# Issue order in a fused attention and two-MoE kernel: casts queued behind bank-emptying additions, and one block's loads on another queue

## The chip, the cores and the metric

The kernel runs on one core of a Trainium2 chip. The core has five instruction streams that run side by side and meet only at semaphores: PE (TensorE, matrix multiplies into PSUM banks), DVE (VectorE), ACT (ScalarE), POOL (GpSimd) and SP (which here only issues DMA transfers). Each stream is served strictly in its own order: an instruction that waits holds up all that stand behind it on that stream. The metric is the time of one execution in microseconds, of which the median of a few runs is shown. A run of this kernel can be told from another when they differ by about 0.2%.

## The reference

Three stages follow one another: attention with rotary embedding over 4 batches of 8 heads, 576 tokens and width 64; a first MoE block; a second one. Only the second matters here:

```python
def _moe2_ref(x, w_in, w_out):          # x: 2304 x 512, w_in: 512 x 2048, w_out: 2048 x 512
    h = x @ w_in
    g = h * (1.0 / (1.0 + np.exp(-h)))
    return (g @ w_out).astype(np.float32)
```

## The kernel before

Every float32 matrix is held as two float16 parts, a high one (`h`, an ACT cast with a scale) and a low one (`l`, what the cast left over, made by DVE's scalar_tensor_tensor from the source and `h`). A product is three passes: high by high, high by low, low by high.

The second MoE (`moe2`, from line 871) takes the 2304 tokens in 9 blocks of 256, numbered `jb` 0 to 8. Block 0 is alone: `s1(u)` computes its hidden values with plain products, for four units u of 512 hidden values. Blocks 1 and 2, 3 and 4, 5 and 6, 7 and 8 go in pairs, J = 0 to 3 (`A` is the odd block, `B` the even one). For a pair, `s1_pair(J, p)`, p = 0 to 7, forms a 2 by 2 block product with seven multiplications (`PRODUCTS`) in place of eight. Their inputs are seven linear forms of x, cast into the tile `yr` by `y7_forms`; form b is written over tile place b from place b + 1, so that the forms can only be made one after another. Seven products of six passes each are 42 matmuls of 256 columns, into four PSUM banks a, b (ring `m`) and c, d (ring `mb`).

Then the banks are emptied: ACT copies one half of b and one half of c (lines 953 and 957), DVE makes six additions and POOL one (lines 952 and 960), and ACT applies SiLU in place (line 964). Until the additions that read a bank are done, the next step can't write to it.

`second(jb, u)` is the product with w_out for one unit, again 42 matmuls (`s2`, line 1010). It needs the unit's hidden values in seven forms: `g_split` makes four sums on POOL (`gsum`, line 893) and two casts each on ACT (line 897) and DVE (line 898). `splits()` calls `g_split` for units that are complete, up to three ahead of the next `second`. After the four units of a block, `close(jb)` combines and stores it.

For each J the next pair's operands are brought in meanwhile: `y7_load(J + 1)` (four DMAs of 256 KB out of the scratch `yscr`, traced in step p = 0), `y7_max` (the greatest magnitude, one DVE reduction, line 150, p = 1), `y7_sums` (the scale, by two small PE operations and a row of small DVE ones, and four POOL differences, line 981; p = 2), `y7_forms` (p = 3 to 7). For J = 0 all this stands in the loop over `s1`.

The order of each engine's instructions is not the order of the program text. A planner simulates the kernel and lets each engine take, at each moment, a ready instruction, the earliest traced one first. `tc.issue_after(ins)` binds the instructions traced inside it: those on the engine of `ins` stand behind `ins` in that engine's order. It adds no wait for the end of `ins`. On its own, a cast whose input is ready early may be set ahead of the additions of a step that was traced before it.

Of the kernel before, what the change touches and what calls it, by code (L numbers as in the profile page):

```python
# [7 lines left out]
F32 = mybir.dt.float32  # L8
# [3 lines left out]
AF = mybir.ActivationFunctionType  # L12
ALU = mybir.AluOpType
# [4 lines left out]
P = 128  # L18
# [4 lines left out]
def fused_kernel(  # L23
# [22 lines left out]
    nc = tc.nc  # L46
# [102 lines left out]
    def absmax(out, in_):  # L149
        nc.vector.tensor_reduce(out=out, in_=in_, op=ALU.max, axis=AX.X, apply_absolute_value=True)  # L150

    def flat(t):
        return t.rearrange("p a b -> p (a b)")

    def split(h, l, x, s, engine="act", later=False):

        if engine == "act":
            nc.scalar.activation(out=h, in_=x, func=AF.Copy, scale=s)  # L158
        elif engine == "pool":
            last["pool"] = nc.gpsimd.tensor_scalar(out=h, in0=x, scalar1=s, scalar2=1.0, op0=ALU.mult, op1=ALU.mult).ins  # L160
        else:
            nc.vector.tensor_scalar(out=h, in0=x, scalar1=s, scalar2=None, op0=ALU.mult)
        low = lambda: nc.vector.scalar_tensor_tensor(out=l, in0=x, scalar=s, in1=h, op0=ALU.mult, op1=ALU.subtract)
        return low if later else low()
# [3 lines left out]
    class Weights:  # L168
# [12 lines left out]
        def place(self, pool):  # L181
            n, m, nm = self.n, self.m, self.nm
            self.first = pool.tile([P, n], F16, name=nm + "f")
            self.all = pool.tile([P, m * n], F32, name=nm)
            self.t = [self.all[:, i * n:(i + 1) * n] for i in range(m)]
# [63 lines left out]
    last = {}  # L249
# [241 lines left out]
    for i, (b, hp) in enumerate(pairs):  # L491
        u = first[b, hp]
# [232 lines left out]
        W.scale("s" + nm, n=M)  # L725
        yield

    def y_load(jb, t, n):

        for i in range(n // 256):  # L730
            o = (jb + i) * 256
            if n == 256:
                nc.sync.dma_start(out=t[:, 0:2].rearrange("p a (c n) -> p (a c) n", c=2), in_=yscr[:, :, o:o + 256])
            else:
                for a in range(2):
                    nc.sync.dma_start(
                        out=t[:, 1 - i + 2 * a].rearrange("p (c n) -> p c n", c=2), in_=yscr[:, 2 * a:2 * a + 2, o:o + 256]
                    )
        return t
# [131 lines left out]
    def moe2(st, pools, rings, ps_a, wo_rest, w7, w8_load):  # L871
# [4 lines left out]
        turn, w8 = [0], [w8_load(k) for k in range(4)]  # L876
        total = HB * (1 + nb // 2)

        def w8_next():
            k = turn[0]  # L880
            turn[0] += 1
            return w8[k]
# [5 lines left out]
        def g_split(jb, u, g):  # L888

            sm = sum_p.tile([P, 4, 256], F32, tag="gsum", name="gsum")  # L890
            q = [g[:, i] for i in range(4)] + [sm[:, i] for i in range(4)]
            for o, x, y, op in SUMS:
                nc.gpsimd.tensor_tensor(out=q[o], in0=q[x], in1=q[y], op=op)  # L893
            t = g7[jb, u] = g7_p.tile([P, 2, 7, 2, P], F16, tag="g7", name="g7")
            for lo, hi, x in ((0, 3, flat(g[:, 1:4])), (3, 7, flat(sm))):
                h, l = (t[:, i, lo:hi].rearrange("p a i n -> p (a i n)") for i in range(2))
                nc.scalar.activation(out=h, in_=x, func=AF.Copy, scale=sg_t[jb])  # L897
                nc.vector.scalar_tensor_tensor(out=l, in0=x, scalar=sg_t[jb], in1=h, op0=ALU.mult, op1=ALU.subtract)  # L898

        def s1(u):  # L900
            yt, _, ch, _ = st["y0"]
# [21 lines left out]
        def s1_pair(J, p):  # L923
# [25 lines left out]
            tm = tm_p.tile([P, 4, 256], F32, tag="t1", name="t1")  # L949
            place = lambda g, i: g[:, 2 * i:2 * i + 2, e * P:e * P + P]  # L950
            two = lambda x: x.rearrange("p (t n) -> p t n", t=2)
            add = lambda o, x, y: nc.vector.tensor_tensor(out=o, in0=x, in1=y, op=ALU.add)  # L952
            nc.scalar.activation(out=tm[:, 0], in_=b[:, 0], func=AF.Copy)
            add(tm[:, 1], a[:, 0], tm[:, 0])
            add(place(ga, 1), two(a[:, 1]), two(tm[:, 0]))
            add(tm[:, 0], b[:, 1], tm[:, 1])
            nc.scalar.activation(out=tm[:, 2], in_=c[:, 0], func=AF.Copy)
            add(place(ga, 0), two(c[:, 1]), two(tm[:, 0]))
            add(tm[:, 3], tm[:, 1], tm[:, 2])
            nc.gpsimd.tensor_tensor(out=place(gb, 0), in0=two(tm[:, 0]), in1=two(tm[:, 2]), op=ALU.add)  # L960
            add(place(gb, 1), two(d[:, 0]), two(tm[:, 3]))
            for g in (ga, gb):
                x = g[:, :, e * P:e * P + P]
                nc.scalar.activation(out=x, in_=x, func=AF.Silu, scale=ch)
# [1 line left out]
                ready[A, u], ready[B, u] = ga, gb  # L966

        def y7_load(J):
            return y_load(1 + 2 * J, yr_p.tile([P, 8, 512], F32, tag="yr", name="yr"), 512)

        def y7_max(r):
            m = small.tile([P, 1], F32, tag="ym", name="ym")
            absmax(m, flat(r[:, 0:4]))
            return m

        def y7_sums(J, r, m):
# [7 lines left out]
        def y7_forms(J, r, s, ch, lo_hi=range(7)):  # L984
            for b in lo_hi:
                t = r[:, b].bitcast(F16)
                split(t[:, 0:512], t[:, 512:1024], r[:, b + 1], s)
            if lo_hi[-1] == 6:
                sc[J] = [r[:, b].bitcast(F16).rearrange("p (x c n) -> p x c n", x=2, c=2) for b in range(7)], ch

# [64 lines left out]
        def second(jb, u):  # L1055
            splits()
            s2(jb, u)
            used[0] += 1
            splits()
            if u == UNITS - 1:  # L1060
                close(jb)
# [14 lines left out]
                y7_forms(0, raw, *y7_sums(0, raw, m))  # L1076
        second(0, 1)
        rest_step(99)
        todo = [(0, u) for u in range(2, UNITS)]
        for J in range(nb // 2):  # L1080
            A, B = 1 + 2 * J, 2 + 2 * J
            more = J + 1 < nb // 2
# [194 lines left out]
```

## Time and profile before

| what | value |
|---|---|
| median of 3 runs | 1036.11 us (1034.75 to 1036.45) |
| the profiled execution | 1035.59 us |
| its span, first to last instruction | 1033.9 us |
| mean granted TensorE clock | 0.976 of full speed |
| PE busy | 962.4 us, 93% of the span |
| DVE, ACT, POOL busy | 688.3, 616.3, 489.6 us |
| second MoE, first to last matmul | 682.3 to about 1028.5 us of the span |

The profiled execution's own time is 1.7 us above its span, and 0.5 us under the median. All of the change lies in the last third of the span. "Busy" of an engine counts its instructions from start to end; matmuls overlap, so counting them in a stretch says more about PE than its busy share.

### The profile page before, as it was taken

The page shows a single profiled execution, that of the slowest core. Times are in us where ns is not written, and L with a number is a line of the kernel's source. Part 1 is how long each engine was busy: PE and PEld are TensorE (multiplying, and loading weights), DVE is VectorE, ACT ScalarE, POOL GpSimd, SP SyncE. Part 2 cuts the span into 40 slices and gives each one's busy share as a digit, 9 for nine tenths or more (in the row PEclk, how much of TensorE's full clock was granted, in tenths as well). Part 3 has the DMA queues.
Part 4 walks back from the last instruction along what each step waited for, and adds up shares of the span by engine and source line. Part 5 has one row for each costly group of instructions (what it writes and reads, how often), then busy time and mean ns, then how long its engine had stood idle before and what let it go on. Part 6 is the DMA issues. An engine that isn't in the chain of part 4 may idle for free.

```text
span 1033.9 us, 19511 instructions
## 1 busy us (share of the span) xinstructions
PE 962.4 (93%) x7234; PEld 717.0 (69%) x7234; DVE 688.3 (67%) x1295; ACT 616.3 (60%) x1377; POOL 489.6 (47%) x548
## 2 busy tenths in 40 slices
PE   4677998999999999998999999999999999999997
PEld 2343664666666766655756668777888888888887
DVE  6769877765567655687566646645678767867454
ACT  3778676566666575867767754534455644644352
POOL 6735593961127720354223205536258457346164
PEclk9688999999999999999999999999999999999999
DMA  6943132422334510653444415254345244342201
GB/s 152 280 115 101 33 97 75 129 71 62 102 109 110 137 47 27 189 147 118 144 123 139 143 58 168 82 187 145 128 144 168 92 152 125 108 129 93 90 3 41
DMA packets 126062, 117.99 MB, mean 114 GB/s; under 512 B 47376, under 2 KB 109584, under 8 KB 125968
## 3 DMA queue, kind: packets, MB, share of 16 engines
q1 hardware_dynamic: 124464, 116.03, 37.4%
q8 instruction: 57, 0.93, 0.4%
q10 hardware_dynamic: 1504, 0.72, 0.3%
q14 instruction: 37, 0.30, 0.1%
HBM read 90.51 MB, written 26.21 MB: 113 GB/s over the span
## 4 chain that ended last, share of the span: by engine, by line
PE 62%; DVE 9%; ACT 6%; POOL 6%; DMA 6%; issue 3%; SPq 1%; ACTq 0%; DVEq 0%; POOLq 0%
PE m L538 18%; PE xp L467 6%; PE m L946 5%; PE s L390 5%; PE tr L448 5%; PE mb L946 4%; POOL gsum L893 4%; PE mg L538 3%; PE c L1010 3%; PE a L1010 2%; PE b L1010 2%; POOL yr L981 2%; DVE nb L400 1%; PE d L1010 1%; DVE g L898 1%
## 5 line engine op out<-in xcount | busy, mean ns | idle before, releaser
L538 PEld LDWEIGHTS <-w 128*128 128x128 f16 x1632 | 157.3, 98 | 68.8 <-issue 27.8
L538 PE MATMUL m<-x,w 128*128 128x256 f16 (+1 forms) x1336 | 189.7, 288 | 9.9 <-ACT t L554 4.0
L1010 PEld LDWEIGHTS <-g 128*128 128x128 f16 x1485 | 145.7, 98 | 19.9 <-issue 2.3
L946 PEld LDWEIGHTS <-w8s 128*128 128x128 f16 x1344 | 131.4, 98 | 20.3 <-issue 4.8
L400 DVE TENSOR_REDUCE nb<-s 128x2 f32<-128x1152 f32 (+1 forms) x80 | 98.7, 1234 | 49.4 <-PE s L390 39.5
L212 POOL TENSOR_SCALAR z<-z 128x256 uint16<-128x256 uint16 x64 | 56.0, 875 | 159.2 <-DVE z L211 148.4
L407 ACT ACTIVATE e<-s,nb 128x576 f32<-128x576 f32 x144 | 105.1, 735 | 29.0 <-DVE nb L400 24.9
L419 ACT ACTIVATE e<-e,rec 128x576 f32<-128x576 f32 x144 | 104.5, 768 | 17.8 <-DVE rec L417 17.5
L448 PE MATMUL tr<-ident,e 128*128 128x128 f32 x576 | 97.4, 289 | 14.2 <-ACT T L350 6.2
L787 POOL TENSOR_TENSOR z<-z 128x128 f32<-128x128 f32 (+1 forms) x96 | 59.0, 634 | 105.5 <-DMA z<-zwo 38.4
L448 PEld LDWEIGHTS tr<-ident,e 128*128 128x128 f32 x576 | 69.8, 147 | 50.0 <-issue 13.4
L946 PE MATMUL m<-yr,w8s 128*128 128x256 f16 x768 | 90.8, 273 | 3.7 <-DVE t L952 3.7
L452 ACT ACTIVATE pt<-tr 128x384 f32<-128x384 f32 x119 | 56.8, 486 | 47.9 <-PE tr L448 47.7
L467 PE MATMUL xp<-pt,vd 128*64 128x256 f32 (+1 forms) x512 | 84.6, 419 | 0.0
L390 PE MATMUL s<-T 64*128 64x512 f32 x256 | 83.7, 698 | 0.0
L960 POOL TENSOR_TENSOR z<-t 128x256 f32<-128x256 f32 x32 | 28.0, 875 | 95.8 <-DVE t L952 55.9
L946 PE MATMUL mb<-yr,w8s 128*128 128x256 f16 x576 | 69.9, 274 | 2.3 <-ACT yr L158 2.1
L538 PE MATMUL m<-h,wo 128*128 128x256 f16 (+1 forms) x448 | 64.9, 286 | 0.1
L898 DVE SCALAR_TENSOR_TENSOR g<-gsum,sg,g 128x1024 f16<-128x1024 f32 x36 | 49.1, 1373 | 22.1 <-ACT g L897 21.6
L538 PEld LDWEIGHTS <-wo 128*128 128x128 f16 x512 | 49.3, 98 | 16.9 <-issue 4.0
L897 ACT ACTIVATE g<-gsum,sg 128x1024 f16<-128x1024 f32 x36 | 40.7, 1140 | 32.8 <-POOL gsum L893 32.8
L330 POOL TENSOR_TENSOR w<-qk,sin_sb 128x384 f32<-128x384 f32 (+1 forms) x44 | 45.7, 1058 | 30.4 <-DMA qk<-in_q_dram 16.0
(231 smaller groups left out, 1910.8 us busy)
## 6 DMA issues: line engine op xcount, KB each, us to landing
w8s<-w8scr SPq DMA_DIRECT2D x64, 448.0 KB, 4.2
z<-in_moe_w_in_dram SPq DMA_DIRECT2D x32, 256.0 KB, 3.2
z<-in_moe_w_out_dram SPq DMA_DIRECT2D x32, 256.0 KB, 3.3
w<-in_moe_w_dram SPq DMA_DIRECT2D x6, 768.0 KB, 6.0
wo<-in_moe_w_dram SPq DMA_DIRECT2D x6, 768.0 KB, 4.6
qk<-in_q_dram SPq DMA_DIRECT2D x32, 128.0 KB, 3.0
vd<-in_v_dram SPq DMA_DIRECT2D x16, 256.0 KB, 3.0
zwi<-z SPq DMA_DIRECT2D x32, 128.0 KB, 3.1
```

The lines of the kernel that those rows point to most:

```text
L390: last["s"] = nc.tensor.matmul(s[:, o:o + 512], qs[r], kt[r], start=True, stop=True).ins
L400: x = nc.vector.tensor_reduce(out=nb[:, 0:m], in_=both(s, 0, 960, 576) if m > 1 else s[:, 0:576], op=ALU.max, axis=AX.X, negate=True)
L407: x = nc.scalar.activation(out=e[:, HK[g]], in_=s[:, SK[g]], func=AF.Exp, bias=nb[:, g:g + 1], accum_out=sm[:, g:g + 1])
L419: nc.scalar.activation(out=e[:, HK[g]], in_=e[:, HK[g]], func=AF.Copy, scale=r[:, g:g + 1])
L448: nc.tensor.transpose(tr[:, i * n:(i + 1) * n], e[0:n, c * P:(c + 1) * P], ident[0:n, 0:n])
L452: nc.scalar.activation(out=to, in_=of, func=AF.Copy)
L467: nc.tensor.matmul(xp[r, 0:n], v4[:, g, c, :], pt[:, c + 5 * g, :], start=False, stop=(c == 3))
L538: nc.tensor.matmul(ps[:, 0:n], l, r, start=(first and i == 0), stop=(not more and i == len(passes) - 1))
L787: nc.gpsimd.tensor_tensor(out=z[:, o], in0=z[:, x], in1=z[:, y], op=op)
L898: nc.vector.scalar_tensor_tensor(out=l, in0=x, scalar=sg_t[jb], in1=h, op0=ALU.mult, op1=ALU.subtract)
L946: nc.tensor.matmul(o, l, r, start=(i == 0), stop=(i == len(passes) - 1))
L1010: x = nc.tensor.matmul(ps, l, r, start=first, stop=last_, skip_group_check=True)
```

## The change

Three things are changed in `moe2`.

1. A helper `behind(k)` binds what is traced inside it behind `last[k]`, if that has been set. `last["sa"]` is the ACT copy of bank c and `last["sv"]` the last DVE addition (bank d) of the latest `s1_pair`. Bound in this way are the ACT casts and the DVE casts in `g_split` and in `y7_forms`, and the DVE reduction in `y7_max`. Before the first `s1_pair` neither is set, and nothing is bound.
2. `second(0, 2)` is traced ahead of the first `s1_pair`; before, it came behind it.
3. The four loads of `y7_load(0)` are issued by ScalarE's queue, those of the other pairs by SP's as before.

```diff
-    def y_load(jb, t, n):
+    def y_load(jb, t, n, queue=nc.sync):
...
-                    nc.sync.dma_start(
+                    queue.dma_start(
...
+        def behind(k):
+            return tc.issue_after(last[k]) if k in last else nullcontext()
+
...  g_split
-                nc.scalar.activation(out=h, in_=x, func=AF.Copy, scale=sg_t[jb])
-                nc.vector.scalar_tensor_tensor(out=l, in0=x, scalar=sg_t[jb], in1=h, op0=ALU.mult, op1=ALU.subtract)
+                with behind("sa"):
+                    nc.scalar.activation(out=h, in_=x, func=AF.Copy, scale=sg_t[jb])
+                with behind("sv"):
+                    nc.vector.scalar_tensor_tensor(out=l, in0=x, scalar=sg_t[jb], in1=h, op0=ALU.mult, op1=ALU.subtract)
...  s1_pair
-            add = lambda o, x, y: nc.vector.tensor_tensor(out=o, in0=x, in1=y, op=ALU.add)
+            add = lambda o, x, y: nc.vector.tensor_tensor(out=o, in0=x, in1=y, op=ALU.add).ins
...
-            nc.scalar.activation(out=tm[:, 2], in_=c[:, 0], func=AF.Copy)
+            last["sa"] = nc.scalar.activation(out=tm[:, 2], in_=c[:, 0], func=AF.Copy).ins
...
-            add(place(gb, 1), two(d[:, 0]), two(tm[:, 3]))
+            last["sv"] = add(place(gb, 1), two(d[:, 0]), two(tm[:, 3]))
...  y7_load, y7_max, y7_forms
-            return y_load(1 + 2 * J, yr_p.tile([P, 8, 512], F32, tag="yr", name="yr"), 512)
+            return y_load(1 + 2 * J, yr_p.tile([P, 8, 512], F32, tag="yr", name="yr"), 512, nc.sync if J else nc.scalar)
...
-            absmax(m, flat(r[:, 0:4]))
+            with behind("sv"):
+                absmax(m, flat(r[:, 0:4]))
...
-                split(t[:, 0:512], t[:, 512:1024], r[:, b + 1], s)
+                with behind("sa"):
+                    nc.scalar.activation(out=t[:, 0:512], in_=r[:, b + 1], func=AF.Copy, scale=s)
+                with behind("sv"):
+                    nc.vector.scalar_tensor_tensor(
+                        out=t[:, 512:1024], in0=r[:, b + 1], scalar=s, in1=t[:, 0:512], op0=ALU.mult, op1=ALU.subtract
+                    )
...  moe2's loop
         second(0, 1)
         rest_step(99)
-        todo = [(0, u) for u in range(2, UNITS)]
+        second(0, 2)
+        todo = [(0, u) for u in range(3, UNITS)]
```

## Rows read from the trace of the kernel before

**Rows 1.** Windows: length; busy (count) PE, PEld, DVE, ACT, POOL; clock; DMA
```profile
692.00:702.00 10.00, 8.62 (x80) 7.47 (x79) 5.81 (x5) 3.14 (x5) 10.00 (x10) 1.00 0.76 236
...
714.00:727.00 13.00, 10.68 (x81) 8.56 (x79) 7.87 (x9) 6.77 (x9) 2.77 (x3) 0.87 0.04 15
727.00:785.00 58.00, 58.00 (x532) 51.81 (x530) 43.45 (x83) 32.85 (x54) 31.39 (x32) 1.00 0.48 155
785.00:812.00 27.00, 24.67 (x223) 21.31 (x221) 20.37 (x38) 12.92 (x20) 19.85 (x22) 1.00 0.39 123
...
870.00:886.00 16.00, 14.04 (x128) 12.04 (x125) 12.14 (x19) 7.57 (x12) 9.45 (x10) 1.00 0.50 149
886.00:1028.00 142.00, 142.00 (x1302) 127.22 (x1301) 88.88 (x149) 66.55 (x101) 67.18 (x77) 1.00 0.24 74
```

**Rows 2.** Timeline of PE: start, us, instruction, [idle before <- releaser]
```profile
714.74 0.82 PE L946 MATMUL m<-yr,w8s 128*128 128x256 f16 x6
...
720.54 0.27 PE L946 MATMUL mb<-yr,w8s 128*128 128x256 f16 x1 [2.13 <-ACT yr L158]
...
729.63 1.36 PE L1010 MATMUL a<-w,g 128*128 128x256 f16 x11
...
779.28 2.78 PE L946 MATMUL m<-yr,w8s 128*128 128x256 f16 x24
...
789.17 2.78 PE L946 MATMUL m<-yr,w8s 128*128 128x256 f16 x24 [0.56 <-DVE t L952]
...
799.91 2.78 PE L946 MATMUL m<-yr,w8s 128*128 128x256 f16 x24 [1.41 <-DVE t L952]
...
876.17 2.78 PE L946 MATMUL m<-yr,w8s 128*128 128x256 f16 x24 [1.69 <-DVE t L952]
```

**Rows 3.** Windows of 5 us, columns as in the first group
```profile
690.00:695.00 5.00, 3.62 (x34) 3.00 (x33) 4.49 (x3) 2.80 (x4) 4.88 (x4) 1.00 1.08 352
...
720.00:725.00 5.00, 4.46 (x26) 3.37 (x26) 3.36 (x4) 1.96 (x4) 0.00 (x0) 0.66 0.01 3
```

**Rows 4.** Timeline of ACT, sixth and seventh cast of pair 0's forms
```profile
723.44 0.72 ACT L158 ACTIVATE yr<-yr,sh 128x512 f16<-128x512 f32 x1 [0.82 <-DVE yr L163]
724.98 0.72 ACT L158 ACTIVATE yr<-yr,sh 128x512 f16<-128x512 f32 x1 [0.82 <-DVE yr L163]
```

**Rows 5.** Timeline of DVE: a last form, then 776 to 798
```profile
725.73 0.75 DVE L163 SCALAR_TENSOR_TENSOR yr<-yr,sh 128x512 f16<-128x512 f32 x1 [0.79 <-ACT yr L158]
...
776.18 0.42 DVE L952 TENSOR_TENSOR z<-mb,t 128x256 f32<-128x256 f32 x1
...
784.59 2.27 DVE L150 TENSOR_REDUCE ym<-yr 128x1 f32<-128x2048 f32 x1
786.79 0.41 DVE L952 TENSOR_TENSOR t<-m,t 128x256 f32<-128x256 f32 x1
...
795.47 2.88 DVE L898 SCALAR_TENSOR_TENSOR g<-gsum,sg,g 128x1024 f16<-128x1024 f32 x2
```

**Rows 6.** Timeline of POOL: two of pair 0's differences, one addition
```profile
688.07 1.27 POOL L981 TENSOR_TENSOR yr<-yr 128x512 f32<-128x512 f32 x1 [21.50 <-DMA yr<-yscr]
690.12 4.44 POOL L981 TENSOR_TENSOR yr<-yr 128x512 f32<-128x512 f32 x3 [0.78 <-DMA yr<-yscr]
...
791.84 0.90 POOL L960 TENSOR_TENSOR z<-t 128x256 f32<-128x256 f32 x1
```

**Rows 7.** Timeline of the DMA issue queues, SP and ScalarE's
```profile
682.72 1.46 SPq L736 DMA_DIRECT2D yr<-yscr  x3
684.28 0.89 SPq L581 DMA_DIRECT2D yscr<-y  x2
685.22 2.74 SPq L736 DMA_DIRECT2D yr<-yscr  x5
...
2.17 0.65 ACTq L280 DMA_DIRECT2D qk<-in_k_dram  x1
```

**Rows 8.** The loads of yr, all sixteen: issue to landing
```profile
DMA to landing us min/median/max: 2.9/5.2/6.6
```

## Prediction

> **What bounds the kernel now.** I read the windows of the second MoE first, since the change touches nothing before it. From 727 to 785 us 532 matmuls are recorded in 58 us, and from 886 to 1028 1302 in 142 us: 9.17 per us both times, 0.109 us for each [rows 1]. The reader should take this as PE's full pace; where it holds, no other order of casts can gain anything. Four stretches fall short of it. 692 to 702 has 80 where 91.7 would fit: 11.7 x 0.109 = 1.3 us lost. 714 to 727 has 81 where 119.2 would fit: 4.2 us. 785 to 812 has 223 for 247.7: 2.7 us. 870 to 886 has 128 for 146.8: 2.0 us [rows 1]. Together 10.2 us. That is all that the change can win, and it would end at 1026.
>
> The second view is PE's timeline, to see what ended each hole. In the 714 to 727 stretch PE stood 2.13 us for an ACT cast of pair 0's forms [rows 2], and then ran at a mean granted clock of 0.66 from 720 to 725, between the levels of 1.2 and 2.4 GHz, with 26 matmuls in those 5 us [rows 3]. At 789.17, 799.91 and 876.17 it stood 0.56, 1.41 and 1.69 us for a DVE addition that empties a bank [rows 2]. The third view is the timeline of the engines named: at 784.59 DVE starts the 2.27 us reduction of `y7_max` and reaches the additions of step (1, 0) only at 786.79, and casts of units occupy it from 795.47 for 2.88 us with the additions of step (1, 1) behind them [rows 5]. That is what part 1 is about: work that is not urgent, ahead of additions on which PE waits.
>
> **The binding.** It removes no instruction and adds none; it shifts ACT and DVE work. Each cast must be asked behind which step it was traced. `y7_max(2)` is traced in step (1, 1), so it now stands behind that step's additions. The additions of (1, 0) can then follow the cast that ends at about 784.6, 2.2 us sooner [rows 5], and the 0.56 us hole at 789.17 goes [rows 2]. The casts at 795.47 are those of units (B, 1) and (B, 2). By the count in `splits()` they are traced in steps (0, 7) and (1, 0), and the binding puts them behind those two, not behind (1, 1), which they hold up. So the 1.41 us hole, and the like one of 1.69 us, need not go. POOL is also full there, 19.85 of 27 us [rows 1]: it reaches an addition of step (1, 0) at 791.84 only [rows 6], with differences and sums ahead of it that the change leaves as they are. The bounds for the two boundaries are 0 and 2.7 + 2.0 = 4.7 us won. I take 1.0: the 0.56, and a little of the rest for additions that come sooner.
>
> What the shifted work costs: the reduction for pair 1 comes into the stretch 727 to 785, where DVE is busy 43.45 of 58 us [rows 1]; 14.5 us are free for 2.27. I cost it at nothing. If DVE's free time lies in the wrong places there, PE would lose at most those 2.27 us. In the last pair no forms are made and PE has no hole, so its order costs and wins nothing [rows 1].
>
> **`second(0, 2)` ahead of pair 0.** The forms come one after another: two ACT casts start 1.54 us apart [rows 4], and the last DVE cast ends at 725.73 + 0.75 = 726.5 [rows 5]. Nothing is bound yet here, so I leave these times. Between 714.74 and 730.83 PE did the 42 matmuls of unit (0, 2), the 42 of step (0, 0) and some 24 of the 42 of unit (0, 3); all 126 would be done at about 730.83 + 18 x 0.109 = 732.8. At the full pace the 126 take 13.7 us and end at 728.5: 4.3 us won at best, if unit (0, 3) fills the waits between forms. With no such filler, (0, 2) ends at 714.74 + 4.58 = 719.3, the step's last product starts at 726.5 and ends at 727.1, and (0, 3) ends at 731.7: 1.1 us won. I take 2.4, between the two, since the planner already mixed (0, 2) into this step [rows 2] and may do so with (0, 3).
>
> **The loads on ScalarE's queue.** Before, three of pair 0's loads were issued from 682.72, then two stores, and the fourth at 685.22 [rows 7]; the second POOL difference, which needs the fourth, began at 690.12 [rows 6]. On ScalarE's queue an issue took 0.65 us [rows 7]: the fourth from about 682.7 + 3 x 0.65 = 684.65, 0.6 us sooner. Landing took 2.9 to 6.6 us [rows 8]. With the least of these the operands would be there at 687.55, 2.6 us sooner; with the greatest at 691.25, 1.1 us later, because the four loads of the next pair, on SP, now travel at the same time. From 690 to 695 the DMA share was already 1.08 at 352 GB/s [rows 3], so I take 0.5 us, the issue time. ACT loses 4 x 0.65 us in a stretch where it only stores y; that I cost at nothing, its cover being PE's work on block 0. The Trainium skill (DMA: Bandwidth & Descriptors, section Issuing engines are not separate DMA queues) speaks against more: transfers started by several engines run on the same 16 DMA engines and interleave, and a second issuer saves only issue time. The full share in the trace agrees. By that rule the sum stays at 1032.2; if two queues did double the rate, it would be near 1030.
>
> **The sum.** 1035.59 for the profiled execution - 2.4 - 1.0 - 0.5 = 1031.7. It stood 0.5 us below the median, so the median after should be **1032.2 us**, 3.9 us or 0.4% faster. About 0.2%, 2.1 us here, is what a measurement of this kernel can tell from no change.
>
> **Rivals.**
> - *Starved step, no change.* With (0, 2) out of the way PE has only a product of 0.65 us for each 1.54 us of forms from 719.3 to 726.5, and no filler. If its clock falls then as it did after the 2.13 us hole, the last product takes 1.3 us, and the stretch behind costs about what 720 to 725 did: 20 matmuls missing x 0.109 = 2.2 us, less the 0.54 us of the hole that lies in it, 1.6 us [rows 3]. The end of (0, 3) moves from 731.7 to 733.9, 1.1 us later than before. Sum: 1036.1 + 1.1 - 1.5 = 1035.7. For it: the clock has fallen at this very place. Against it: the holes would be 0.9 us each, and the clock did not show a fall after single holes of 1.4 and 1.7 us [rows 1, 2]. Also here belongs the plain case that the planner's new order moves the holes without closing them.
> - *All holes close.* 4.3 here, 4.7 at the boundaries less a bit: 8 us, 1028. For it: each hole has a cast or a reduction in front. Against it: POOL.
> - *Late form, slower.* Form 6 of the next pair is traced in step 7 and is now behind that step's last addition, at 776.18 for J = 0 [rows 5]. Step (1, 0) starts at 779.28 [rows 2] and needs form 6 in its sixth product, 30 x 0.109 = 3.3 us on, at 782.6. If the planner lets the casts of units go first, which filled DVE to 784.59 [rows 5], form 6 ends at 785.3 and PE waits 2.8 us. The same order stands at all three boundaries: 8.4 us against a gain of 3.9, 1040.6. It decides from 2.0 us at each. Against it: a form is a short cast (0.75 us) that is ready at once, and two units of 4.6 us each can lie between the steps.
>
> **Chances.** Forecast, 1029.5 to 1034.0: 0.50. All holes, below 1029.5: 0.12. No change, 1034.0 to 1038.2: 0.25. Late form, above: 0.13. So faster 0.62, same 0.25, slower 0.13. From 1028.0 to 1038.0 leaves out about half of the second case and the last one, under 2 in 10; the forecast's own range is 1029.5 to 1034.0.
>
> **What would show it.** PE's timeline: no stop for a form cast of over 1 us before step (0, 0) and no clock row of 0.66 behind it; in DVE's timeline no line 150 or form ahead of additions of the step they were traced in; the hole at 789 gone, those before step 2 of pairs 1 and 2 still there, smaller. The fourth load issued about 0.6 us sooner and landing no faster. The prediction is wrong if PE waits for forms of line 946 at the start of pairs 1 to 3, if the clock row falls for longer, or if holes appear within 727 to 785, where there was none.

## The result, and the profile after

The change made the kernel slower: 1044.51 us (median of 8 runs, 1042.5 to 1048.83) against 1037.45 us for the kernel before (8 runs beside them, 1034.39 to 1042.1). The ratio is 1.0068, with a 95% interval of 1.0046 to 1.0089. The forecast was 1032.2 us and its range ended at 1038.0, so the time lies outside the range, on the side to which 13 in 100 had been given.

The profiled execution after took 1045.29 us. The head of its page:

```profile
span 1043.6 us, 19517 instructions
...
PE 968.7 (93%) x7234; PEld 719.2 (69%) x7234; DVE 697.2 (67%) x1295; ACT 616.5 (59%) x1377; POOL 493.5 (47%) x548
```

The span grew by 9.7 us, from 1033.9. Not all of that is the change's. The second MoE's first matmul came at 682.3 us in the profile of before and at 686.2 in that of after, although no engine's order differs ahead of it; over the profiles of all kernels here it came between 680.7 and 691.2. I therefore compare from that matmul to the end of the span and call this **the stage**: 1033.9 - 682.3 = 351.6 us before, 1043.6 - 686.2 = 357.4 us after, 5.8 us more.

To see where, both profiles are cut into the same stretches, counted from that first matmul: A is its first 52 us (block 0 and the start of pair 0), B from 52 to 95 us (the middle of pair 0), C from 95 to 140 us (the boundary of pairs 0 and 1), D from 180 to 215 us (the boundary of pairs 1 and 2). The windows of before, which cut otherwise than [rows 1]; columns as there:

```profile
682.30:734.30 52.00, 48.24 (x420) 41.57 (x418) 26.15 (x36) 23.50 (x32) 26.45 (x25) 0.97 0.55 182
734.30:777.30 43.00, 43.00 (x394) 38.37 (x393) 32.92 (x71) 25.06 (x42) 23.04 (x26) 1.00 0.47 151
777.30:822.30 45.00, 42.67 (x387) 37.43 (x386) 35.90 (x58) 23.96 (x37) 32.44 (x32) 1.00 0.40 130
...
862.30:897.30 35.00, 33.04 (x300) 29.03 (x298) 24.36 (x48) 18.88 (x30) 20.44 (x25) 1.00 0.38 121
```

The same windows after, and below them two short ones that are used further on:

```profile
686.20:738.20 52.00, 47.86 (x420) 41.26 (x418) 26.77 (x38) 23.49 (x32) 27.75 (x26) 0.97 0.57 182
738.20:781.20 43.00, 41.91 (x380) 36.72 (x379) 32.57 (x65) 22.99 (x39) 19.05 (x23) 1.00 0.45 144
781.20:826.20 45.00, 41.08 (x359) 35.46 (x357) 34.48 (x56) 21.49 (x32) 30.17 (x30) 0.96 0.38 124
866.20:901.20 35.00, 32.16 (x291) 28.00 (x289) 25.84 (x45) 14.94 (x24) 22.20 (x23) 1.00 0.33 95
...
712.00:717.00 5.00, 4.18 (x23) 2.89 (x24) 4.12 (x4) 4.04 (x6) 3.76 (x5) 0.67 0.61 224
815.00:820.00 5.00, 5.00 (x31) 3.73 (x31) 0.98 (x5) 3.31 (x4) 0.63 (x1) 0.66 0.01 3
```

The reader counts matmuls. At the full pace of 9.17 per us a stretch could hold length x 9.17; each that is missing is 0.109 us lost. A: 476.8 - 420 = 56.8, 6.2 us, in both kernels alike. B: 394.3 - 394 = 0 before, 394.3 - 380 = 14.3 after, 1.6 us. C: 412.7 - 387 = 25.7 before, 2.8 us; 412.7 - 359 = 53.7 after, 5.8 us. D: 321.0 - 300 = 21.0 before, 2.3 us; 321.0 - 291 = 30.0 after, 3.3 us. So the change costs 0 + 1.6 + 3.0 + 1.0 = 5.6 us, nearly all of the stage's 5.8. The stretches between and behind (140 to 180 and from 215 us) run at full pace in both.

PE's waits from 686.2 us to the end, after (in total, times, longest):

```profile
PE m L117 <- DVE t L957: 4.3, 2, 3.1
PE b L1019 <- ACT g L901: 3.1, 1, 3.1
PE m L951 <- DVE t L957: 2.4, 2, 1.6
PE m L951 <- DVE ga L957: 0.9, 1, 0.9
```

And PE's timeline after, of the steps and holes that answer to [rows 2]:

```profile
712.69 0.28 PE L1019 MATMUL b<-w,g 128*128 128x256 f16 x1 [3.12 <-ACT g L901]
...
757.28 2.78 PE L951 MATMUL m<-yr,w8s 128*128 128x256 f16 x24 [0.90 <-DVE ga L957]
...
794.06 2.78 PE L951 MATMUL m<-yr,w8s 128*128 128x256 f16 x24
...
804.20 2.78 PE L951 MATMUL m<-yr,w8s 128*128 128x256 f16 x24 [0.81 <-DVE t L957]
...
811.40 0.38 PE L1021 MATMUL c<-w,g 128*128 128x256 f16 x2
814.90 0.27 PE L117 MATMUL m<-ident,ym 128*1 128x128 f32 x1 [3.12 <-DVE t L957]
815.01 1.29 PE L1021 MATMUL c<-w,g 128*128 128x256 f16 x10
```

Four things stand there. The stop for a form cast (2.13 us in [rows 2]) is gone, and a stop of 3.12 us at 712.69, for a cast of unit (0, 0), has come in its place. Step (1, 1), at 794.06, starts without a hole, where there were 0.56 us; at step (1, 2) 0.81 us are left of 1.41. Behind it is a new hole of 3.12 us, at 814.90: there the transposition of pair 2's maximum (line 117) needs an `m` bank, and it stands in PE's order ahead of the rest of unit (B, 1), which could have run. And at 757.28 PE stands 0.90 us within pair 0, where there had been no hole at all. The granted clock is 0.66 from 815 to 820, behind the 3.12 us, between the levels of 1.2 and 2.4 GHz. Before, PE waited only 0.37 us for this transposition:

```profile
807.21 0.27 PE L117 MATMUL m<-ident,ym 128*1 128x128 f32 x1 [0.37 <-DVE t L952]
```

In stretch C, PE's waits thus come to 0.56 + 1.41 + 0.37 = 2.3 us before and 0.81 + 3.12 = 3.9 us after. The rest of the 3.0 us more that C loses goes with the lower clock.

What DVE did ahead of the two new holes (its timeline, after):

```profile
742.88 2.28 DVE L150 TENSOR_REDUCE ym<-yr 128x1 f32<-128x2048 f32 x1
...
806.37 0.41 DVE L957 TENSOR_TENSOR z<-mb,t 128x256 f32<-128x256 f32 x1
806.70 2.27 DVE L150 TENSOR_REDUCE ym<-yr 128x1 f32<-128x2048 f32 x1
808.89 1.37 DVE L903 SCALAR_TENSOR_TENSOR g<-z,sg,g 128x768 f16<-128x768 f32 x1
812.07 1.36 DVE L903 SCALAR_TENSOR_TENSOR g<-gsum,sg,g 128x1024 f16<-128x1024 f32 x1 [1.80 <-ACT g L901]
813.35 0.41 DVE L957 TENSOR_TENSOR t<-m,t 128x256 f32<-128x256 f32 x1
```

The reduction of `y7_max` now starts the moment the additions of the step in which it was traced are done: at 742.88 behind step (0, 1), at 806.70 behind step (1, 1). Before, that of pair 2 ran at 784.59, ahead of the additions of (1, 0) [rows 5]. The work is the same and has only changed its place: it no longer stands ahead of (1, 0)'s additions, but ahead of those of (1, 2), which start at 813.35 behind the reduction and two casts of block B's units. The second of these casts waits 1.80 us for ACT's half, and ACT for POOL's sums, so that POOL's sums came last at this hole; what the reduction added to it is read from e1 below. ACT's timeline:

```profile
711.48 1.15 ACT L901 ACTIVATE g<-gsum,sg 128x1024 f16<-128x1024 f32 x1 [6.42 <-POOL gsum L896]
...
810.88 1.15 ACT L901 ACTIVATE g<-gsum,sg 128x1024 f16<-128x1024 f32 x1 [2.24 <-POOL gsum L896]
```

### The profile page after: what moved, and what is told of

It reads as the page before. It is cut to its first block, busy times and chain, and to the rows that moved or that the text cites. A ratio compares the mean times of both kernels' runs of the same rounds, so it can differ in the third digit from the quotient of the medians.

```text
span 1043.6 us, 19517 instructions
## 1 busy us (share of the span) xinstructions
PE 968.7 (93%) x7234; PEld 719.2 (69%) x7234; DVE 697.2 (67%) x1295; ACT 616.5 (59%) x1377; POOL 493.5 (47%) x548
## 4 chain that ended last, share of the span: by engine, by line
PE 61%; DVE 8%; POOL 4%; ACT 4%; DMA 4%; issue 3%; SPq 1%; ACTq 0%; DVEq 0%; POOLq 0%
PE m L538 17%; PE xp L467 6%; PE m L951 5%; PE s L390 5%; PE tr L448 4%; PE mb L951 4%; PE mg L538 3%; PE c L1021 3%; PE a L1021 3%; PE b L1021 3%; POOL gsum L896 2%; DMA yr<-yscr 2%; POOL yr L987 2%; PE d L1021 2%; PE xp L463 1%
## 5 line engine op out<-in xcount | busy, mean ns | idle before, releaser
L903 DVE SCALAR_TENSOR_TENSOR g<-gsum,sg,g 128x1024 f16<-128x1024 f32 x36 | 52.7, 1466 | 22.8 <-ACT g L901 22.2
L467 PEld LDWEIGHTS xp<-pt,vd 128*64 128x64 f32 x512 | 36.7, 138 | 34.4 <-issue 17.4
```

The costliest lines, as they stand in the source:

```text
L467: nc.tensor.matmul(xp[r, 0:n], v4[:, g, c, :], pt[:, c + 5 * g, :], start=False, stop=(c == 3))
```

## The experiments

**My theory** after the result: the bound reduction is the main cost; 2.3 us of DVE's time directly behind a step's additions push everything behind it, and what PE waits for is the next step's additions. **The first rival**: it is the planner's new order as a whole (casts, `second(0, 2)`, loads), the reduction being one among several. **The second rival**: the loads, which land later on the other queue, delay pair 0 and all that follows. A third question came up on the way: whether POOL, which the prediction took as fixed, is the real limit at the boundaries.

The table gives all runs: the ratio to the kernel before measured beside them, the stage, and the us that PE loses in stretches A to D, worked out as above. The stage and the losses come from one profiled execution each, and the losses by stretch differ by some 2 us between kernels with the same holes, where the clock falls behind a hole or does not; the ratios come from 5 to 10 runs each.

| kernel | ratio (95%) | stage us | A | B | C | D |
|---|---|---|---|---|---|---|
| before | 1 | 351.6 | 6.2 | 0.0 | 2.8 | 2.3 |
| after, the whole change | 1.0068 (1.0046 to 1.0089) | 357.4 | 6.2 | 1.6 | 5.8 | 3.3 |
| e2, reduction bound alone | 1.0038 (1.0021 to 1.0056) | 352.4 | 4.1 | 1.1 | 4.2 | 2.6 |
| e3, loads alone | 1.0000 (0.9983 to 1.0017) | 351.5 | 5.8 | 0.0 | 2.8 | 2.6 |
| e4, second(0, 2) first alone | 1.0009 (0.9989 to 1.0029) | 351.0 | 4.7 | 0.1 | 3.3 | 2.4 |
| e6, forms bound alone | 0.9988 (0.9966 to 1.0010) | 352.6 | 4.7 | 0.6 | 4.4 | 2.4 |
| e1, after without the reduction bound | 1.0020 (1.0004 to 1.0036) | 353.3 | 5.9 | 0.1 | 4.1 | 2.6 |
| e8, after with loads on SP | 1.0069 (1.0040 to 1.0099) | 357.6 | 5.4 | 1.6 | 6.0 | 4.0 |
| e14, e1 with loads on SP | 1.0015 (0.9996 to 1.0035) | 351.3 | 4.1 | 0.1 | 4.2 | 2.5 |
| e13, after with a halved reduction | 1.0031 (1.0008 to 1.0054) | 354.3 | 5.5 | 0.3 | 4.3 | 3.8 |
| e17, after with the reduction twice | 1.0052 (1.0026 to 1.0077) | 356.4 | 5.4 | 3.3 | 3.7 | 3.3 |
| e9, after with the scales a step later | 1.0040 (1.0017 to 1.0062) | 352.7 | 5.3 | 0.5 | 4.5 | 1.8 |
| e10, before with POOL's differences bound | 0.9929 (0.9906 to 0.9952) | 343.6 | 1.9 | -0.1 | 1.3 | -0.1 |
| e11, e10 with second(0, 2) first | 0.9921 (0.9896 to 0.9945) | 344.6 | 2.3 | 0.4 | 1.4 | 0.0 |
| e12, after with POOL's differences bound | 1.0007 (0.9985 to 1.0029) | 350.3 | 4.0 | 1.6 | 4.1 | 0.0 |
| e15, e12 without the reduction bound | 0.9959 (0.9936 to 0.9981) | 346.7 | 4.3 | 0.1 | 1.6 | 0.0 |
| e16, e10 with the reduction bound | 0.9959 (0.9936 to 0.9982) | 346.9 | 2.7 | 0.7 | 3.1 | -0.1 |

### The reduction: taken out of the change, and done alone (e1, e2)

e1 is the kernel after with this edit:

```diff
-            with behind("sv"):
-                absmax(m, flat(r[:, 0:4]))
+            absmax(m, flat(r[:, 0:4]))
```

> The changed kernel with the reduction of y7_max free again, all else as changed. Stage from the first matmul of s1 to the end of the span: 351.6 us before, 357.4 changed. Theory 1 (the bound reduction puts 2.3 us of DVE work between the additions of step 1 and those of step 2, and PE's transposition for the maximum waits on the bank): stage 352 to 353, time within 0.2% of before, no stop of PE of 3.1 us for the transposition near 812. Theory 2 (the bound casts of the forms come late): stage stays 356 to 358, time 0.5% slower or more. Theory 3 (the loads on ScalarE's queue and the 3.1 us hole near 712 are the cost): the hole near 712 stays and the stage is at least 3 us longer than before.

e2 is the kernel before with the opposite edit and nothing else.

> The kernel before with the reduction of y7_max bound, nothing else changed. Theory 1: new holes before step 2 or 3 of pairs 1 and 2 and in step 3 of pair 0, stage 355 to 357.5, 0.3 to 0.6% slower than before. Theories 2 and 3: stage 351 to 352.5, within 0.2% of before.

Measured: freeing the reduction takes the loss from 0.68% to 0.20% (1.0020, 1.0004 to 1.0036); binding it alone costs 0.38% (1.0038, 1.0021 to 1.0056). It is the largest part, by both ways of asking. The stages agree less well. That of e1, 353.3, lies just above the range that its expectation gave to this theory. That of e2, 352.4, lies in the range given to the other theories, and only its ratio fits this one: stretch A lost 2.1 us less in e2's profile than in that of before, which hides the 2.8 us more lost in B to D (7.9 us against 5.1). DVE and PE of e1 at the same boundary, and its window behind the hole:

```profile
807.58 0.41 DVE L957 TENSOR_TENSOR z<-mb,t 128x256 f32<-128x256 f32 x1
809.89 1.58 DVE L903 SCALAR_TENSOR_TENSOR g<-z,sg,g 128x768 f16<-128x768 f32 x1 [1.90 <-ACT g L901]
813.27 1.35 DVE L903 SCALAR_TENSOR_TENSOR g<-gsum,sg,g 128x1024 f16<-128x1024 f32 x1 [1.80 <-ACT g L901]
```

```profile
796.95 2.78 PE L951 MATMUL m<-yr,w8s 128*128 128x256 f16 x24 [1.41 <-DVE t L957]
...
806.11 2.78 PE L951 MATMUL m<-yr,w8s 128*128 128x256 f16 x24
...
816.10 0.27 PE L117 MATMUL m<-ident,ym 128*1 128x128 f32 x1 [2.40 <-DVE t L957]
```

```profile
815.00:820.00 5.00, 3.90 (x34) 3.37 (x35) 2.58 (x8) 3.12 (x4) 0.73 (x1) 1.00 0.03 11
```

Behind step (1, 1)'s additions DVE now has no reduction, but it stands idle for 1.90 us instead, waiting for ACT's half of a cast, and then 1.80 us more for the cast whose sums POOL makes, as long as in the kernel after. The hole at line 117 shrinks only from 3.12 to 2.40 us, and one of 1.41 us stands again ahead of step (1, 1). Together that is 3.8 us of waits in stretch C, against 3.9 with the reduction bound and 2.3 before. So at this boundary the reduction ran almost wholly in time in which DVE would have waited for POOL and ACT; what made PE's waits longer than before lies in the other parts of the change. The difference between after and e1 in C, 1.7 us, is the clock: 0.66 behind the hole of 3.12 us, 1.00 behind that of 2.40. In stretch B, on the other hand, the loss of 1.6 us vanishes (0.1): in the middle of pair 0 the reduction is the whole cause.

In e2 the hole stands at another place. Its DVE, and its PE:

```profile
809.07 2.27 DVE L150 TENSOR_REDUCE ym<-yr 128x1 f32<-128x2048 f32 x1
```

```profile
807.87 4.11 PE L949 MATMUL m<-yr,w8s 128*128 128x256 f16 x24 [2.10 <-DVE t L955]
```

There PE waits 2.10 us before step (1, 2), in place of 2.3 us in three holes, and the 24 matmuls behind the hole take 4.11 us where 24 take 2.78 elsewhere: the granted clock was 0.75 from 810 to 815.

### The other parts alone (e3, e4, e6)

Each is the kernel before with one hunk of the change:

```diff
e3
-            return y_load(1 + 2 * J, yr_p.tile(...), 512)
+            return y_load(1 + 2 * J, yr_p.tile(...), 512, nc.sync if J else nc.scalar)
e4
-        todo = [(0, u) for u in range(2, UNITS)]
+        second(0, 2)
+        todo = [(0, u) for u in range(3, UNITS)]
e6
-                split(t[:, 0:512], t[:, 512:1024], r[:, b + 1], s)
+                with behind("sa"):
+                    nc.scalar.activation(out=t[:, 0:512], in_=r[:, b + 1], func=AF.Copy, scale=s)
+                with behind("sv"):
+                    nc.vector.scalar_tensor_tensor(...)
```

> The kernel before with the first pair's four loads on ScalarE's queue, nothing else. Theory 3: the operands land later because the next pair's four loads travel beside them, POOL's first differences begin 9 us after the first matmul of s1 in place of 5.8, a hole of 2 to 4 us before unit (0, 0), stage 353.5 to 356. Theories 1 and 2: landing may be later but the form hole near 720 takes it up, stage within 1 us of 351.6.

> The kernel before with the third product of block 0 traced ahead of the first step, nothing else. The prediction's step: 1 to 4 us won between 714 and 733, stage 348 to 350.5. Rival (the planner only moves the hole): stage within 1 us of 351.6 and a hole of about 2 us elsewhere before the first step's end.

> The kernel before with the casts of the forms bound, nothing else (bound alone, the casts of the units leave every engine's order as it was). Theory 2 (late forms or casts): stage 353.5 or more against 351.6 before, 0.2% slower or more, with stops of PE for casts at the start of pairs 1 to 3. Theory 1 (the reduction alone): stage 351 to 352, time within 0.15% of before.

Measured: 1.0000, 1.0009 and 0.9988; each interval holds 1. None of the three can be told from no change when it stands alone. The stages of e3 and e4 fit that; e6's, 352.6, lies between its two ranges, since the clock fell to 0.75 (800 to 805 us) behind a hole of 2.00 us before step (1, 2). The fourth part, the casts of `g_split` bound alone, gives the same order as before on every engine; there was nothing to run. The kernel after without this binding has the same orders as with it, too, so that it has no share in the loss.

### Loads back on SP's queue (e8, e14)

e8 is the kernel after with the loads of pair 0 issued by SP again; e14 is e8 with the reduction free as well, so that what is left of the change is the bound casts and `second(0, 2)`.

```diff
-            return y_load(1 + 2 * J, yr_p.tile(...), 512, nc.sync if J else nc.scalar)
+            return y_load(1 + 2 * J, yr_p.tile(...), 512)
```

> The changed kernel with the first pair's loads back on SP's queue. If the hole of 3.1 us before unit (0, 0) comes from the loads and is what is left beside the reduction: stage 354 to 355.5 against 357.4 changed, time 0.4 to 0.5% above before. If the loads only change which hole it is: stage 356.5 to 358, time as of the changed kernel, with a hole for a form near 720 in place of the other.

> The changed kernel with the reduction free and the loads on SP's queue: what stays is the binding of the casts and the earlier third product. If the rest beside the reduction (0.2%) is the loads': stage 350.5 to 352, time within 0.15% of before. If it is the casts or the order: stage 353 or more, 0.2% slower.

Measured: e8 1.0069 (1.0040 to 1.0099), like the whole change with its 1.0068; e14 1.0015 (0.9996 to 1.0035), like e1 with its 1.0020. No effect of the loads can be told on either side, and the second rival falls as the main cause. The stage of e14, 351.3, does lie in the range that its expectation gave to the loads, 2.0 us under that of e1; but 1.8 us of that are stretch A, where the clock was 0.66 behind e1's hole (715 to 720 us) and 1.00 behind e14's (724 to 729). The loads do move the hole in stretch A: with loads on ScalarE's queue (after, e3) PE stands for a unit's sum and cast, with loads on SP (before, e4, e8) for a form cast of 2.1 to 2.6 us. With them on ScalarE's queue A loses 5.3 to 6.2 us (six kernels, 5.7 in the mean), on SP's 4.1 to 6.2 (six, 4.9), leaving aside the five kernels with POOL's differences bound; a cost of the loads of under 1 us is not excluded.

### The price by the reduction's length (e13, e17)

Two sizes of the reduction, for pairs 1 to 3, in the kernel after. e13 leaves half of the operands out of the maximum; e17 does the reduction a second time.

```diff
e13
-                absmax(m, flat(r[:, 0:4]))
+                absmax(m, flat(r[:, 0:2 if "sv" in last else 4]))
e17
                 absmax(m, flat(r[:, 0:4]))
+                if "sv" in last:
+                    absmax(m, flat(r[:, 0:4]))
```

> The changed kernel with the bound reduction cut to half of its elements for pairs 1 to 3 (half of the operands is left out of the maximum), 1.2 us in place of 2.3. Theory 1, price by length: about half of what freeing the reduction gave, stage 354 to 356, time 0.35 to 0.55% above before. Price by place alone, whatever its length: stage 356.5 to 358.

> The changed kernel with the bound reduction run twice for pairs 1 to 3 (the result is the same). Price by length: three places x 2.3 us more work in front, stage 360 to 365, 1.0 to 1.4% above before. Price by place alone: stage 357 to 359, 0.6 to 0.8% above before.

Measured: in stretch B PE loses 0.1 us with no reduction there (e1), 0.3 with half, 1.6 with the whole, 3.3 with two. There it is the length that counts, less nearly half a reduction (1.21 us in e13) that fits. In stretch C the row is 4.1, 4.3, 5.8, 3.7: no rule. The hole at line 117 is as long with half the reduction as with the whole; e13's PE:

```profile
810.34 0.27 PE L117 MATMUL m<-ident,ym 128*1 128x128 f32 x1 [3.12 <-DVE t L957]
```

Behind it the clock stayed at 1.00 (810 to 815 us), where it was 0.66 in the kernel after and in e8; that is the difference between 4.3 and 5.8. With the reduction twice the hole is 2.46 us. The ratio of e13, 1.0031 (1.0008 to 1.0054), is near what the price by length would be; that of e17, 1.0052 (1.0026 to 1.0077), is not above that of the change, and its stage of 356.4 is below both ranges of its expectation. So at the boundary it isn't the reduction's length that sets the hole, and a theory by which each us on DVE costs one of PE fails there.

### The scales a step later (e9)

The 3.12 us hole is the transposition of `y7_sums`, which needs an `m` bank. e9 is the kernel after with `y7_sums` traced in step p = 3 and the forms from p = 4.

```diff
-                if p == 2 and more:
+                if p == 3 and more:
                     sums = y7_sums(J + 1, raw, m)
-                if p > 2 and more:
-                    y7_forms(J + 1, raw, *sums, lo_hi=((0,), (1,), (2, 3), (4, 5), (6,))[p - 3])
+                if p > 3 and more:
+                    y7_forms(J + 1, raw, *sums, lo_hi=((0, 1), (2, 3), (4, 5), (6,))[p - 4])
```

> The changed kernel with y7_sums traced one step later (p = 3) and the forms from p = 4, so that PE's transposition for the maximum does not stand before step 2's banks are empty. If half of theory 1's price is PE waiting with the transposition in front of work that it could do: stop of 3.1 us near 812 falls to 1.5 or less, stage 354 to 355.5 against 357.4 changed. If the price is the reduction ahead of the additions alone: stage stays 356 to 358.

Measured: 1.0040 (1.0017 to 1.0062). The hole at line 117 is gone and C loses 4.5 us instead of 5.8; the kernel is still slower than before. The stage, 352.7, is below both ranges of the expectation, but the interval of the ratio overlaps that of the change, so that a gain of the move isn't shown. PE's waits in C still come to 3.7 us, at other lines: the transposition is where the delay comes out and not where it is made.

### POOL's differences bound (e10, e11, e12)

The prediction had named POOL as full at the boundary, 19.85 of 27 us [rows 1], with the next pair's differences ahead of an addition [rows 6], and left it at that. These kernels bind the four differences as the change binds casts: behind POOL's addition of the step in which they are traced. e10 does this alone to the kernel before, e11 adds `second(0, 2)`, e12 adds it to the whole change.

```diff
-            nc.gpsimd.tensor_tensor(out=place(gb, 0), in0=two(tm[:, 0]), in1=two(tm[:, 2]), op=ALU.add)
+            last["sp"] = nc.gpsimd.tensor_tensor(out=place(gb, 0), in0=two(tm[:, 0]), in1=two(tm[:, 2]), op=ALU.add).ins
...
             for o, x, y in DIFFS:
-                nc.gpsimd.tensor_tensor(out=r[:, o], in0=r[:, x], in1=r[:, y], op=ALU.subtract)
+                with behind("sp"):
+                    nc.gpsimd.tensor_tensor(out=r[:, o], in0=r[:, x], in1=r[:, y], op=ALU.subtract)
```

> The kernel before with POOL's four differences bound behind POOL's addition of the step they are traced in, nothing else. If POOL sets the holes at the boundaries (the prediction's reason why the 1.4 and 1.7 us holes stay): these shrink below 0.5 us each, and the sums of block 0's units come sooner at the start; stage 346 to 349.5 against 351.6, 0.2 to 0.5% faster. If DVE and ACT order alone sets them: stage 351 to 352, time within 0.15%.

> The same with the third product of block 0 traced ahead of the first step as well. If POOL's relief and the order add up: stage 345 to 349, 0.3 to 0.6% faster than before. If the order only moves the hole: within 0.5 us of the stage of the differences alone.

> The changed kernel with POOL's four differences bound behind POOL's addition of their step as well. If the bound reduction costs only because POOL's differences have made the boundary late already: stage 344 to 347, within 1 to 3 us of the differences bound alone (343.6). If it costs by itself: stage 348 or more, with stops of 1 us or more before step 2 of pairs 1 and 2.

Measured: e10 1033.27 us, 0.9929 (0.9906 to 0.9952), and e11 1030.66 us, 0.9921 (0.9896 to 0.9945): both faster than before and after, and not to be told from each other; e10's gain is larger than its expectation's range. e12 comes to 1.0007 (0.9985 to 1.0029), 0.6 points under the change. The windows of e10, stretches A to D:

```profile
686.80:738.80 52.00, 50.81 (x459) 44.24 (x458) 30.10 (x45) 26.91 (x38) 24.94 (x27) 1.00 0.61 201
738.80:781.80 43.00, 43.00 (x395) 38.37 (x393) 32.85 (x64) 24.51 (x40) 26.68 (x28) 1.00 0.50 165
781.80:826.80 45.00, 44.28 (x401) 38.87 (x400) 38.30 (x63) 24.15 (x39) 29.19 (x30) 1.00 0.36 115
...
866.80:901.80 35.00, 35.00 (x322) 31.19 (x320) 27.20 (x51) 18.83 (x30) 16.87 (x17) 1.00 0.41 121
```

and its POOL, first at the start of the stage, then around the boundary of pairs 0 and 1:

```profile
692.49 1.26 POOL L985 TENSOR_TENSOR yr<-yr 128x512 f32<-128x512 f32 x1 [21.24 <-DMA yr<-yscr]
693.99 4.45 POOL L985 TENSOR_TENSOR yr<-yr 128x512 f32<-128x512 f32 x3 [0.24 <-DMA yr<-yscr]
698.39 2.09 POOL L896 TENSOR_TENSOR gsum<-ga 128x256 f32<-128x256 f32 x3
...
789.33 0.72 POOL L963 TENSOR_TENSOR z<-t 128x256 f32<-128x256 f32 x1
...
805.88 0.77 POOL L963 TENSOR_TENSOR z<-t 128x256 f32<-128x256 f32 x1 [2.35 <-DVE t L955]
806.61 5.80 POOL L985 TENSOR_TENSOR yr<-yr 128x512 f32<-128x512 f32 x4
```

At the start the sums of unit (0, 0) follow pair 0's four differences at once; in the kernel before, two of pair 1's came between at 695.89, for 3.20 us, and two more later. At the boundary the four differences of pair 2, 5.80 us together, run at 806.61 behind the addition of step (1, 2); before, the first of them ran at 785.22, with POOL's addition of (1, 0) only at 791.84 [rows 6], 109.5 us after the stage's start. In e10 that addition is at 789.33, 102.5 us after it. Loss D goes to nothing in all five kernels that bind the differences (e10, e11, e12, and e15 and e16 below), whatever else of the change they hold: without the differences' early place nothing of it is left, with the reduction bound or free. The stop of 1 us or more that e12's expectation named came in pair 1 only (1.11 us before step (1, 2), and 1.61 at line 117).

### What is left of the change on that base (e15, e16)

e15 is e12 with the reduction free, e16 is e10 with the reduction bound; both by the edits shown above.

> POOL's differences bound and all of the change but the bound reduction. If the reduction is the cost here too: stage 343.5 to 346.5, 0.5% or more faster than before. If the loads, the order or the bound casts are: stage 348.5 to 351.

> POOL's differences bound and the reduction bound, nothing else of the change. If the reduction costs by itself: stage 347 to 351, with stops of PE for DVE additions or for the transposition before step 2 of pairs 1 and 2. If it needs POOL's congestion: stage 343.5 to 345.5, 0.6% faster than before.

Measured: both 0.9959 (0.9936 to 0.9981 or 0.9982). With e10 at 0.9929 and e12 at 1.0007 this is a square: the reduction bound costs 0.30 points alone and 0.48 on top of the other parts; the other parts cost 0.30 alone and 0.48 on top of the reduction. On top of the other parts the intervals are apart (e12, e15); alone, they overlap a little (e10, e16). PE's hole at line 117 is 1.62 us in e16 and 1.61 in e12; e10 has 0.27 there, e15 none. PE's waits in C come to 0.6 us in e10 and 2.5 in e16, to 1.3 in e15 and 3.5 in e12: once POOL's sums come in time, the reduction adds 1.8 to 2.2 us of waits at this boundary, which in the kernel after POOL's lateness covered. Both stages, 346.7 and 346.9, lie nearer to the range given to the reduction as a cause than to the other. That the other parts cost something together, too, is likely, from e15 against e10 and from e1, whose interval just leaves 1 out; which of them does it isn't settled, since none that ran alone could be told from no change. So the first rival holds for a smaller part of the loss, as far as these ratios tell.

## Why the prediction was wrong

**The step that failed: the binding, and in it the reduction's new place.** The prediction put a gain of 1.0 us on the boundaries, with bounds of 0 and 4.7, and cost the shifted reduction "at nothing", since DVE had 14.5 us free in its new stretch. The stretches show +1.6 us in B, +3.0 in C and +1.0 in D. The 0.56 us hole did go, as forecast, and 1.41 became 0.81. But the lower bound of 0 for the boundaries was no bound: the reduction that had stood ahead of (1, 0)'s additions was moved ahead of (1, 2)'s, where casts that wait for POOL stand as well, and a hole of 3.12 us came there in place of 0.37, with a clock of 0.66 behind it. The length of the hole is mostly not the reduction's: without it PE's waits in C are 3.8 us in place of 3.9 (e1). They are 3.8 us with neither the reduction nor the loads, too (e14), so the bound forms and the earlier `second(0, 2)` together suffice for that; how they do it is open. The prediction asked what the reduction would no longer hold up; it didn't ask what stands behind its new place at the boundaries, and it took POOL's lateness there as given without asking what the new orders would add to it. The reduction's cost was measured four times: 0.48 points (after against e1), 0.38 (e2), 0.48 (e12 against e15) and 0.30 (e16 against e10, the least certain). In us these are 5.0, 3.9, 5.0 and 3.1; the profiles of the same pairs lose 3.9, 2.8, 4.0 and 2.6 us more in B to D. In after against e1 that is 1.5 in B, 0.7 in D, and 1.7 in C by the clock; that the clock falls there in most executions is not shown.

**The 14.5 us of free time.** They were an average. A reduction bound behind a step's additions is ready long before, and starts right behind them (806.70, where the last addition started at 806.37 and takes 0.41 us); DVE's pauses lie elsewhere. The price in B, 1.6 us, is within the 2.27 us that the prediction named as the most; taking nothing was the mistake. e13 and e17 show that nearly half a reduction fits there and most of the rest is PE's loss.

**`second(0, 2)` first: -2.4 us forecast, none measured** (e4, 1.0009; its interval ends at 0.9989, a gain of 1.1 us). The stop for a form before step (0, 0) goes in the kernel after, but stretch A loses 6.2 us as before. The bounds were worked out with the forms' times held fixed and with unit (0, 2) ready at once. In the kernel after, the work that PE was meant to do early was itself late: unit (0, 0) waited until 712.69 for its sums. In e4 the hole of 2.55 us for a form is still there. The starved step, at 25 in 100, was near to this: the holes moved and did not close.

**The loads: -0.5 us forecast, none measured** (e3, e8; the interval of e3 is 1.8 us to either side, too wide to tell 0.5 from nothing). The issue queues after:

```profile
686.40 0.94 ACTq L736 DMA_DIRECT2D yr<-yscr  x2
688.22 0.99 ACTq L736 DMA_DIRECT2D yr<-yscr  x2
...
686.62 1.46 SPq L736 DMA_DIRECT2D yr<-yscr  x3
```

An issue on ScalarE's queue took 0.5 us here, not the 0.65 of [rows 7]. The pair's fourth load went out at 688.22 + 0.99/2 = 688.7, 2.5 us after the stage's start, against 2.9 before: 0.4 us sooner, near the 0.6 forecast. But pair 1's loads go out at the same time from SP. The landings of the eight loads of pairs 0 and 1, before and after:

```profile
DMA to landing us min/median/max: 2.9/4.9/6.3
DMA to landing us min/median/max: 3.5/5.5/7.1
```

All three figures are higher after. DVE's reduction for pair 0, which needs all four loads, starts 9.6 us after the stage's start, against 7.8 before; over all kernels it is 9.4 to 9.8 us with the loads on ScalarE's queue and 7.1 to 8.1 with them on SP's. POOL's first difference came later, too:

```profile
695.36 5.67 POOL L987 TENSOR_TENSOR yr<-yr 128x512 f32<-128x512 f32 x4 [24.73 <-DMA yr<-yscr]
703.07 4.44 POOL L987 TENSOR_TENSOR yr<-yr 128x512 f32<-128x512 f32 x3
...
710.73 0.72 POOL L896 TENSOR_TENSOR gsum<-ga,gsum 128x256 f32<-128x256 f32 x1
```

It starts 695.36 - 686.2 = 9.2 us after the first matmul of the stage; before it was 688.07 - 682.3 = 5.8. Pair 1's operands are there as early as pair 0's, and by the order of the instructions all four of its differences now run ahead of the last of unit (0, 0)'s sums (one among the four at 695.36, two among the three at 703.07, one at 709.51); before, three did. That last sum ends at 711.4; ACT's cast waits 6.42 us for it, and PE 3.12. The Trainium skill (DMA: Bandwidth & Descriptors, section Issuing engines are not separate DMA queues) says that transfers started by several engines share the same DMA engines and interleave; the trace agrees, with 5.5 us as the median landing against 4.9. That sharing can delay the transfer one wants first is what the prediction held as the upper end of its range for this term.

**The rivals.** The late form, with the 13 in 100 for slower, didn't happen: no wait of line 951 for a form stands at the start of pairs 1 to 3, and forms bound alone gave 0.9988. The sign was right by another mechanism, which the list of rivals lacked, though the last sentence of the prediction named its mark: a hole within the stretch where there was none. The closing of all holes was within reach, but not by this change: e10 takes stretches A to D from 11.3 us of loss to 3.0.

**The other signs.** The clock did fall in stretch A, as before, but behind another hole: 0.67 from 712 to 717, around the end of the 3.12 us at 712.69. The reduction stands behind all additions of the step in which it was traced, as forecast. A form need not: one runs at 758.05, ahead of the last addition of its own step (0, 3) at 759.15, since the binding goes by the addition that was traced last (bank d), and the planner had set one of bank c behind it.

## What to carry to other kernels

Binding work behind a step's urgent additions does not make it go into a gap: an instruction that is ready early runs at once where it is bound, and delays the next step's additions by whatever of its length the engine would not have waited there anyway. So a long one (a 2.3 us reduction here) needs a place of its own, chosen from the engine's timeline and not from its free share. When a wait is taken from one step, look up in each engine's order what stands behind the work's new place before its gain is counted. Follow a wait back, engine by engine, to the one that was busy with something less urgent: here the casts waited for POOL's sums, and binding POOL's differences alone won 0.7%, while the change to DVE's and ACT's orders cost 0.7%.

## What the runs showed of the hardware that was not expected

A hole of 2 to 3 us sometimes lowers the granted clock behind it and sometimes doesn't, for the same kind of wait at the same place. The hole of 2.13 us for a form in [rows 2] was followed by a row of 0.66 [rows 3]; in e4 one of 2.55 us for the same form cast left no lower row, and in e8 one of 2.55 us led to 0.74 in the 5 us around its end. The hole of 3.12 us at line 117 was followed by 0.66 in the kernel after and in e8, and by 1.00 in e13. What decides it is not settled here. It makes a single profile's stretches A and C uncertain by some 2 us each (4.1 to 6.2 us lost in A among kernels with such a hole), and is why the verdicts above rest on ratios over many runs.

The start of the second MoE came anywhere from 680.7 to 691.2 us in the profiles, with the same order of instructions ahead of it. This spread of some 10 us is larger than the effect studied, and comparing spans without taking it out would have put 3.9 of the 9.7 us between the two profiles on the change.
